# Gathering x in quarters of rows for three more slots of an attention and expert-layer kernel

## The chip, the core and the metric

The kernel runs on one core of one Trainium2 chip. The metric is the device time of one execution in microseconds (us), as a median over runs. Beside the timed runs there is one execution that the hardware profiler recorded, with the start and length of every instruction on each engine: PE (TensorE, matrix products), DVE (VectorE), ACT (ScalarE), POOL (GpSimd, which also issues the indirect DMAs) and SP (which issues the other DMAs). The program writes one list of instructions for each engine, in an order laid out by hand.

## The reference, cut to what matters

Attention over 8 batches of 576 tokens gives x, 4608 tokens of 512 numbers. Each token then goes to one of 8 experts, and its result is scaled by two gates:

```python
x = np.ascontiguousarray(attn_out.transpose(0, 2, 1, 3)).reshape(B * S, H * D)
...
logits = x @ w_gate
e_idx = np.argmax(logits, axis=1)
...
gate_w = probs[np.arange(N), e_idx]
eom = 1.0 / (1.0 + np.exp(-(x @ w_output_gate)))
...
for e in range(E):
    mask = e_idx == e
    ...
    h = np.maximum(x[mask] @ w1[e], 0.0)
    ye = h @ w2[e]
    out[mask] = gate_w[mask, None] * eom[mask, e, None] * ye
```

`probs` is the softmax of `logits`; w1 takes 512 numbers to 1024 and w2 takes them back.

## The kernel before, in words

**The attention** goes through four pairs of batches. Its x is stored to `xs` in device memory, 4608 rows of 576 numbers: four quarters of 144, each 128 numbers of x and 16 more of which one, written later, is the token's gate.

**The slots.** The expert layer is a list `order` of slots, counted here from 0 as in the code. Slots 0 to 9 take three blocks of 128 tokens each, slots 10 to 13 take two, and further ones, used only if the data needs them, take one. All blocks of a slot belong to one expert. Which tokens a slot takes is found on the chip while the attention still runs: list "a" (slots 0 and 1) after two pairs of batches, list "b" (slots 2 to 4) after three, list "l" (slots 5 and on) after the last. `table` (L213) makes a list: it ends with PE matmuls (L235), a copy `hl` of their result (L242), and the row numbers `idx_g` to gather x by (L249) and `idx_o` to store by (L252). For list "l" it goes on to `idx_q` (L259 to L274): four PE matmuls with the matrix `rep` (L262) spread the row numbers, and four DVE instructions (L267, L269, L272, L274) make from them the numbers of quarter rows. `rep` is made in `settle` (L1258, L1270), which runs once, when the slot with index `LAST` = 1 has been written out and the attention has been finished.

**The gather.** `gather` (L512) fetches a slot's x into a tile `xg`. A slot in `WHOLE` takes one indirect DMA for each block (L525), whole rows, one token on each partition. Any other slot has the flag `quart` and takes four for each block (L519), a quarter of a row each, laid out such that 32 by 32 transposes are enough. So three blocks take 3 issues in the first form and 12 in the second. Before the change `WHOLE` is slots 0 to 5. `gathers` (L587) issues gathers in order, up to two slots past the running one (three `xg` tiles), and only for slots whose flag `listed` is set; where a slot is needed at once (`must`) and is not listed, it calls `force` (L470), which writes out one more step of the list-making until it is.

**Turning x.** The matmuls need x with its columns on the partitions, split into a high and a low part. `turn_x(z, c)` (L1021) does one of four column chunks: for a whole-row slot three PE transposes into a PSUM bank (L1041), for a quarter slot one DVE transpose (L1035); then ACT makes the high part `xh` (L1043) and DVE the low part `xl` (L1044). At the first chunk of a quarter slot ACT also copies the gates out with four small copies (L1031). For slot i + 1 the four chunks are written in slot i, in the second half, after steps 1, 4, 6 and 9 of its 12 (`TURN`, `nxt` in `several`).

**One slot** (`several`, L1160): a first half of 8 matmul groups (L1176), each 12 matmuls into one bank, followed by ACT `hh` (L1181) and DVE `hl` (L1182); a second half of 12 steps of 6 matmuls (L1198) into three banks. As each of the three ends, `finish_y` (L1153) lets ACT scale it into a tile `y` (two buffers) and POOL store it with an indirect DMA (L1156). Weights come by DMA; `split` (L557) divides them into two parts with ACT (L564) and DVE (L565). From `settle` on, ten units of split weights can be held, and the slots' banks rotate through six.

**What else is written between them.** `hook` is called 8 times in the first half and once a step in the second, 20 times a slot. Each call first tries `gathers`, raises a clock by one once the attention is over, and writes two steps of the list-making (`late`): the ranking of the last tokens (`rank`, L875, with the masks `Aw` on POOL, L956), and `route_late` (L338) with list "l" behind it. `hold(n)` waits n ticks of that clock; `take_pr` waits for the one PSUM bank that all list-making shares, until its user clears `taken`.

Of the kernel before, what the change touches and what calls it, by code (L numbers as in the profile page):

```python
# [9 lines left out]
BF16 = mybir.dt.bfloat16  # L10
I32 = mybir.dt.int32
# [5 lines left out]
P = 128  # L17
# [12 lines left out]
NPE = sum(NPS)  # L30
NB3, NB2 = 3 * NPT, 2 * NPP
NBL = NB3 + NB2 + NSS
# [20 lines left out]
LATE = {"lg": 8, "w": 2, "pe": 3, "dve": 2}  # L53
# [1 line left out]
PUMP = (2, 1)  # L55
TURN = {3: (1, 4, 6, 9), 2: (1, 2, 4, 5)}
LAST = 1
WHOLE = tuple(range(NPE + 1))
XQ = 144
XROW = 4 * XQ  # L60

# [5 lines left out]
def attention_moe(tc, phiT, kv, qT, wgo, wall, out):  # L67
# [3 lines left out]
    with contextlib.ExitStack() as ctx:  # L71
        cp = ctx.enter_context(tc.tile_pool(name="cp", bufs=1))
# [20 lines left out]
        idx = {}  # L93
        for nm, n in (("a", 3 * NPS[0]), ("b", 3 * NPS[1]), ("l", NBL)):
            idx[nm] = (cp.tile([P, n], I32, name="idx_g" + nm), cp.tile([P, n], I32, name="idx_o" + nm),
                       cp.tile([P, 4, n], I32, name="idx_q" + nm) if nm == "l" else None)
        slot = cp.tile([P, NSLOT + 1], I32, name="slot")
        ctx.enter_context(tc.manual_schedule())
        ohcs = [cp.tile([P, E], BF16, name=f"ohc{i}") for i in range(NBP)]
# [4 lines left out]
        rt = ctx.enter_context(tc.tile_pool(name="rt", bufs=1))  # L104
# [108 lines left out]
        def table(nm, q, nch, nblk):  # L213

            while nm == "l" and "rl" not in env:
                yield
            bw = (env["rl"] if nm == "l" else rt).tile([P, nch, 2, nblk], BF16, name="bw" + nm)
            w = min(nch, 9 * NBL // nblk // 9 * 9)
            for c in range(0, nch, w):
                b3 = [P, w, nblk]  # L220
                eq = rt.tile([P, 9 * NBL], BF16, name="eq")
                eq = eq[:, 0:w * nblk].rearrange("p (c b) -> p c b", c=w)
                V.tensor_tensor(eq, iota_blk[:, 0:nblk].unsqueeze(1).to_broadcast(b3),
                                q[:, c:c + w].unsqueeze(2).to_broadcast(b3), ALU.is_equal)
                yield
                for i in range(2):
                    V.tensor_tensor(bw[:, c:c + w, i], eq,
                                    tok_hl[:, i, c:c + w].unsqueeze(2).to_broadcast(b3), ALU.mult)
                yield
            yield  # L230
            yield from take_pr()
            yield from hold(LATE["pe"])
            pi = ps_r.tile([P, 2, NBL], F32, name="pr")
            for c in range(nch):
                T.matmul(pi[:, :, 0:nblk], Aw[:, c], bw[:, c], start=(c == 0), stop=(c == nch - 1))  # L235
            yield
            yield from hold(LATE["dve"])
            hl = rt.tile([P, 2, NBL], BF16, name="hl_i")
            iv = rt.tile([P, NBL], F32, name="iv")
            i2 = rt.tile([P, NBL], F32, name="i2")  # L240
            ivv, i2v, hlv = iv[:, 0:nblk], i2[:, 0:nblk], hl[:, :, 0:nblk]
            V.tensor_copy(hlv, pi[:, :, 0:nblk])  # L242
            yield
            V.scalar_tensor_tensor(ivv, hlv[:, 0], 64.0, hlv[:, 1], ALU.mult, ALU.add)
            if nm != "l":
                taken.clear()
            yield
            ig, io, iq = idx[nm]
            V.tensor_scalar(ig[:], ivv, 1.0, 0.0, ALU.subtract, ALU.max)  # L249
            V.tensor_scalar(i2v, ivv, 0.0, 100000.0, ALU.is_equal, ALU.mult)  # L250
            yield
            V.scalar_tensor_tensor(io[:], ivv, -1.0, i2v, ALU.add, ALU.add)  # L252
            if nm != "l":
                return
            for z in order:
                if z["nm"] == nm and not z["quart"]:
                    z["listed"] = True

            rep = env["rep"]  # L259
            pq = ps_r.tile([P, 4, 2, NBL], F32, name="pr")  # L260
            for b in range(4):
                T.matmul(pq[:, b, :, 0:nblk], rep[:, b], hlv, start=True, stop=True)  # L262
            yield
            yield from hold(LATE["dve"])
            t4 = env["rl"].tile([P, 4, NBL], F32, name="iq")
            t4v = t4[:, :, 0:nblk]
            V.tensor_copy(t4v, pq[:, :, 1, 0:nblk])  # L267
            yield
            V.scalar_tensor_tensor(t4v, pq[:, :, 0, 0:nblk], 64.0, t4v, ALU.mult, ALU.add)  # L269
            taken.clear()  # L270
            yield
            V.tensor_scalar(t4v, t4v, 1.0, 0.0, ALU.subtract, ALU.max)  # L272
            yield
            V.tensor_scalar(iq[:], t4v, 4.0, quad[:, 0:1], ALU.mult, ALU.add)  # L274

        def counts(bp):
            pr = ps_r.tile([P, NCH, E], F32, name="pr")
# [3 lines left out]
        def route_early(k):  # L281

            nm, n, s0, nch = "ab"[k], NPS[k], sum(NPS[:k]), (k + 2) * NCH
# [46 lines left out]
            yield  # L330
            yield from table(nm, t1, nch, 3 * n)
            for z in order[s0:s0 + n]:
                z["listed"] = True
            if k == 0:
                gathers(0)
            yield
# [119 lines left out]
        def take_pr():  # L456

            while taken:
                yield
            taken.append(1)  # L460

        def hold(n):

            if "open" not in env:
                return
            end = clock[0] + n
            while clock[0] < end:
                yield
# [29 lines left out]
        for s in range(NSLOT):  # L498
            nb = 3 if s < NPE + NPT else 2 if s < NPE + NPT + NPP else 1
            if s < NPE:  # L500
                k = s >= NPS[0]
                nm, q0, rows = "ab"[k], 3 * (s - NPS[0] * k), (k + 2) * NCH * P
# [463 lines left out]
        def together(*gens):  # L966

            gens = [iter(g) for g in gens]
            while gens:
                for g in list(gens):  # L970
                    try:
                        next(g)
                    except StopIteration:
                        gens.remove(g)
                yield
# [159 lines left out]
        def grow(k):  # L1135
            for r, n in zip((ring, raw, xgs), GROW[k]):
                if n:
                    p = ctx.enter_context(tc.tile_pool(
                        name=f"{r.name}{k + 1}", bufs=n, reuse_waits="tile"))
                    r.add(p, n)  # L1140
# [117 lines left out]
        def settle():  # L1258

            att.finish()  # L1260
            pso.close()
            pa.close()
            env["hs"] = ctx.enter_context(tc.tile_pool(name="hs", bufs=1, side="right", reuse_waits="tile"))
            env["rl"] = ctx.enter_context(tc.tile_pool(name="rl", bufs=1, side="right", reuse_waits="tile"))
            env["xt"] = ctx.enter_context(tc.tile_pool(name="xt", bufs=2, side="right", reuse_waits="tile"))

            env["rep"] = env["rl"].tile([P, 4, P], BF16, name="rep")
            i4 = ident[:].rearrange("p (b i) -> p b i", b=4)
            for b in range(4):
                V.tensor_copy(env["rep"][:, b].rearrange("p (a i) -> p a i", a=4),  # L1270
                              i4[:, b:b + 1].to_broadcast([P, 4, 32]))
            grow(1)
            env["ps"] = ctx.enter_context(tc.tile_pool(name="p1", bufs=7 - NPK, space=PSUM, reuse_waits="tile"))

# [91 lines left out]
```

## Time and profile before

| | |
|---|---|
| Median of 3 timed runs | 578.89 us (578.73 to 579.51) |
| The profiled execution's own time | 577.36 us |
| Its span, first to last instruction | 575.6 us |
| Mean granted TensorE clock | 0.966 |
| Indirect gathers of whole rows | 18 issues |
| Indirect gathers of quarters | 80 issues |
| PE transposes of x (L1041) | 72 |

The profile's first part gives each engine's busy time. The timeline view lists instructions by start time, with their length, engine, line, operation and tiles, a count of merged instructions, and in brackets how long the engine had been idle and what ended that. The windows view gives busy time by stretch, with the granted PE clock. Views by line or by tile give counts, mean lengths, and for DMAs the time from issue to landing.

### The profile page before, as it was taken

Reading aid. Unit: us, or ns where it says so; the run is one execution under the profiler, and the core shown is the slowest. Engines: PE = TensorE matmul, PEld = TensorE weight load, DVE = VectorE, ACT = ScalarE, POOL = GpSimd, SP = SyncE. Lnnn points to the kernel's source line nnn. Section 1 sums busy time; section 2 is a strip of 40 time slices with the busy share of each in tenths; the row PEclk is TensorE's granted clock in tenths of the full one; section 3 lists DMA queues with packets and bytes.
Section 4 is the critical chain, followed back from the end, with each engine's and each line's share of the span. In section 5 each row is a group of like instructions: output and inputs, shape, how many; then the busy total and the mean of one; then the engine's idle time right before and its main releaser. Section 6 shows DMA issues by size and latency. Waiting matters only on the chain. (4 is left out here: it accounts for less than half of the span.)

```text
span 575.6 us, 10886 instructions
## 1 busy us (share of the span) xinstructions
PE 529.1 (92%) x4031; PEld 455.6 (79%) x4031; DVE 356.1 (62%) x736; ACT 280.4 (49%) x496; POOL 229.2 (40%) x253
## 2 busy tenths in 40 slices
PE   3688886789899999999999999999999999999993
PEld 2455554478689799898998989898998989899893
DVE  4485979767765659996443555646465555676610
ACT  3475655454254456453434545445454445656510
POOL 2242575831166034312471735547170604553011
PEclk9987879989899999999999999999999999999998
DMA  8999999975367659756564665656465655687000
GB/s 308 413 401 391 382 376 356 308 301 168 116 197 245 209 173 308 246 155 183 161 200 145 204 177 180 184 171 176 139 202 168 179 172 181 198 264 223 7 28 32
DMA packets 42238, 124.14 MB, mean 216 GB/s; under 512 B 10368, under 2 KB 10432, under 8 KB 41792
## 3 DMA queue, kind: packets, MB, share of 16 engines
q1 hardware_dynamic: 35136, 102.71, 54.7%
q0 software_dynamic: 7040, 20.65, 10.4%
q8 instruction: 33, 0.54, 0.4%
q14 instruction: 29, 0.24, 0.1%
HBM read 102.99 MB, written 20.87 MB: 215 GB/s over the span
## 5 line engine op out<-in xcount | busy, mean ns | idle before, releaser
L1176 PE MATMUL bps<-xh,whl 128*128 128x384 f32 (+1 forms) x896 | 213.6, 322 | 0.1
L1198 PE MATMUL bps<-whl,hh 128*128 128x512 f32 x608 | 197.7, 396 | 0.0
L565 DVE TENSOR_TENSOR whl<-w,whl 128x1024 fp32r<-128x1024 f32 x112 | 136.8, 1228 | 68.5 <-ACT whl L564 68.5
L1176 PEld LDWEIGHTS bps<-xh,whl 128*128 128x128 f32 x896 | 156.9, 190 | 1.9 <-issue 0.6
L1176 PE MATMUL bps<-xl,whl 128*128 128x384 f32 (+1 forms) x448 | 143.8, 321 | 0.0
L1198 PEld LDWEIGHTS bps<-whl,hh 128*128 128x128 f32 x608 | 114.7, 189 | 26.1 <-issue 2.5
L1198 PE MATMUL bps<-whl,hl 128*128 128x512 f32 x304 | 119.0, 391 | 0.0
L564 ACT CAST whl<-w 128x1024 fp32r<-128x1024 f32 x112 | 116.4, 1046 | 0.0
L519 POOL DMA_INDIRECT xg<-xs,idx_ql x80 | 90.2, 1127 | 25.2 <-issue 24.3
L1181 ACT ACTIVATE hh<-bps 128x384 fp32r<-128x384 f32 (+1 forms) x96 | 48.9, 510 | 96.9 <-PE bps L1176 96.7
L1182 DVE SCALAR_TENSOR_TENSOR hl<-bps,hh 128x384 fp32r<-128x384 f32 (+1 forms) x96 | 55.1, 577 | 52.1 <-ACT hh L1181 52.1
L1176 PEld LDWEIGHTS bps<-xl,whl 128*128 128x128 f32 x448 | 85.1, 190 | 0.5
L1156 POOL DMA_INDIRECT out<-y,idx_ol x23 | 24.9, 1081 | 127.1 <-ACT y L1155 101.4
L1198 PEld LDWEIGHTS bps<-whl,hl 128*128 128x128 f32 x304 | 57.5, 189 | 10.8
L838 POOL TENSOR_TENSOR ea<-ea,mx 128x512 f32<-128x512 f32 (+1 forms) x20 | 19.2, 961 | 49.8 <-DVE mx L836 45.4
L1043 ACT CAST xh<-xt 128x384 fp32r<-128x384 f32 (+1 forms) x32 | 14.7, 460 | 37.9 <-DVE xt L1035 37.9
L873 ACT COPY xo<-bpd 128x576 f32<-128x576 f32 x36 | 22.6, 640 | 21.3 <-PE bpd L871 12.7
L956 POOL TENSOR_SCALAR Aw<-iota_row,row 128x128 bf16<-128x128 bf16 x36 | 26.8, 759 | 12.4 <-DVE row L946 12.4
L871 PE MATMUL bpd<-ve_b,aT 64*128 64x144 f32 (+1 forms) x320 | 28.5, 327 | 2.4 <-DVE ea L833 2.4
L1044 DVE TENSOR_TENSOR xl<-xt,xh 128x384 fp32r<-128x384 f32 (+1 forms) x32 | 15.8, 492 | 24.1 <-ACT xh L1043 24.1
L1155 ACT ACTIVATE y<-bps,gx 128x512 f32<-128x512 f32 x20 | 13.4, 687 | 30.4 <-PE bps L1198 13.9
L871 PEld LDWEIGHTS bpd<-ve_b,aT 64*128 64x128 f32 (+1 forms) x320 | 21.7, 196 | 8.1 <-issue 3.5
(248 smaller groups left out, 471.6 us busy)
## 6 DMA issues: line engine op xcount, KB each, us to landing
w<-wall SPq DMA_DIRECT2D x112, 512.0 KB, 3.9
kvt<-kv SPq DMA_DIRECT2D x32, 512.0 KB, 7.5
xs<-xo SPq DMA_DIRECT2D x16, 576.0 KB, 5.8
qt<-qT SPq DMA_DIRECT2D x16, 512.0 KB, 9.1
ph<-phiT SPq DMA_DIRECT2D x3, 1152.0 KB, 12.1
kv<-kv SPq DMA_DIRECT2D x4, 512.0 KB, 9.0
xg<-xs,idx_ql POOLq DMA_INDIRECT x80, 4.2
ph<-phiT SPq DMA_DIRECT2D x4, 288.0 KB, 3.2
```

Source lines behind the costliest of these rows:

```text
L519: G.indirect_dma_start(out=z["xg"][:, k, XQ * b:XQ * b + XQ], out_offset=None, in_=xs[0:z["rows"]].rearrange("t (a q) -> (t a) q", a=4), i ...
L564: A.copy(hl[:, 0], w[:])
L565: V.tensor_tensor(hl[:, 1], w[:], hl[:, 0].bitcast(F32), ALU.subtract)
L838: G.tensor_tensor(eav, eav, mx[:, 0:n].unsqueeze(2).to_broadcast([P, n, M]), ALU.subtract)
L871: T.matmul(px[to:to + n, r, sl], z["aT"][h, o:o + n], ves[2 * bp + b][h, g], start=True, stop=True)
L873: A.copy(xo[:, c % 2], px[:, :, 0:2 * XQ])
L956: (G if AWP else V).tensor_scalar(Aw[:, bp * NCH + c], iota_row[:], row[:, c:c + 1], None, ALU.is_equal)
L1156: G.indirect_dma_start(out=out, out_offset=bass.IndirectOffsetOnAxis(ap=z["idx"][1][:, z["q0"] + k:z["q0"] + k + 1], axis=0), in_=y[:], in ...
L1176: T.matmul(pb[:, j % pb.shape[1], 0:n_], w[:, b, o:o + P], x[a][:, cc, 0:n_], start=(n == 0), stop=(n == 11))
L1181: A.activation(h_[:, js, 0:n_], pb[:, :, 0:n_], AF.Relu)
L1182: V.scalar_tensor_tensor(l_[:, js, 0:n_], pb[:, :, 0:n_], 0.0, h_[:, js, 0:n_].bitcast(F32), ALU.max, ALU.subtract)
L1198: T.matmul(py[k], h[u - 4][a][:, f, k * P:(k + 1) * P], w[:, b, DM * f:DM * f + DM], start=(u == 4 and f == 0 and n == 0), stop=(u == 7 an ...
```

## The change

Slots 3, 4 and 5 (the fourth to the sixth) become quarter slots too, so `WHOLE` is now 0, 1, 2. List "b" gets its own `idx_q`. The making of quarter numbers, until now the tail of `table`, becomes a generator `quarters(nm, hlv)` of its own. For list "l" it is still run at the end of `table`. For list "b" it needs `rep`, so `settle` puts it beside the ranking that is then under way (`together` lets each of the two go one step at a time), and the copy `hl` of list "b", in a tile of its own, is kept for it. A quarter slot is `listed` only when its quarter numbers have been written out.

```diff
-WHOLE = tuple(range(NPE + 1))
+WHOLE = (0, 1, 2)
...
-                       cp.tile([P, 4, n], I32, name="idx_q" + nm) if nm == "l" else None)
+                       cp.tile([P, 4, n], I32, name="idx_q" + nm) if nm != "a" else None)
...
-            hl = rt.tile([P, 2, NBL], BF16, name="hl_i")
+            hl = rt.tile([P, 2, nblk], BF16, name="hl_i" + nm)
...
             V.scalar_tensor_tensor(io[:], ivv, -1.0, i2v, ALU.add, ALU.add)
+            if nm == "b":
+                hls[nm] = hlv
             if nm != "l":
                 return
             for z in order:
                 if z["nm"] == nm and not z["quart"]:
                     z["listed"] = True
-
+            yield from quarters(nm, hlv)
+
+        hls = {}
+
+        def quarters(nm, hlv=None):
+
+            if hlv is None:
+                yield from take_pr()
+                yield from hold(LATE["pe"])
+                hlv = hls[nm]
+            iq, nblk = idx[nm][2], hlv.shape[2]
             rep = env["rep"]
             pq = ps_r.tile([P, 4, 2, NBL], F32, name="pr")
             for b in range(4):
...
             V.tensor_scalar(iq[:], t4v, 4.0, quad[:, 0:1], ALU.mult, ALU.add)
+            for z in order:
+                if z["nm"] == nm:
+                    z["listed"] = True
...
             for z in order[s0:s0 + n]:
-                z["listed"] = True
+                z["listed"] = z["listed"] or not z["quart"]
...
+            late.gens[0:1] = [together(quarters("b"), *late.gens[0:1])]
             grow(1)
```

## The prediction

> **What bounds the kernel now.** I read the engines' busy times first, then the windows view over the stretch that the change touches, then the timeline of each engine there.
>
> ```profile
> span 575.6 us, 10886 instructions
> PE 529.1 (92%) x4031; PEld 455.6 (79%) x4031; DVE 356.1 (62%) x736; ACT 280.4 (49%) x496; POOL 229.2 (40%) x253
> 212.00:248.50 36.50, 36.50 (x193) 33.30 (x192) 35.11 (x102) 21.48 (x32) 15.67 (x16) 1.00 0.82 268
> ```
>
> The last line is, roughly, slot 2: start and end, length, then busy time of PE, PEld, DVE, ACT and POOL, and the granted clock. PE has no gap, so a PE instruction less is time less. But DVE is busy for 35.11 of these 36.50 us as well (whole-kernel share: 62%), because `late` makes list "l" there.
>
> ```profile
> 241.22 0.33 PE L1176 MATMUL bps<-xh,whl 128*128 128x384 f32 x1
> 277.48 0.33 PE L1176 MATMUL bps<-xh,whl 128*128 128x384 f32 x1
> 308.90 0.49 PE L1041 MATMUL bps<-ident,xg 128*128 128x128 f32 x3
> 311.98 0.33 PE L1176 MATMUL bps<-xh,whl 128*128 128x384 f32 x1
> 345.01 0.33 PE L1176 MATMUL bps<-xh,whl 128*128 128x384 f32 x1
> ```
>
> The L1176 rows are the first matmuls of slots 3, 4, 5 and 6. Slot 5 already turns a quarter slot, slot 6: 345.01 - 311.98 = 33.03 us. Slot 4 turns a whole-row slot with four groups of PE transposes: 34.50. Slot 3 has those and list "l"'s matmuls: 36.26, so 1.76 for the list.
>
> **What it takes away.** The four groups for slots 3, 4 and 5, which stand in slots 2, 3 and 4: 34.50 - 33.03 = 1.47 us each, 4.4 in all. A group shows 0.49 us, but matmuls overlap, so I take the difference of slot times. In the Trainium skill, page "VectorE: DVE Perf Modes", section "The three transpose paths", a 128x128 transpose is put at 390 ns on TensorE, and the page's rules advise TensorE for it, which speaks against the change. By 390 ns the 24 transposes of slots 3 and 4 would free 9.4 us, not 2.9, and my sum would be 6.4 lower; the trace disagrees, with three of them in 0.49 us.
>
> **What it adds: when slot 3's x arrives.** The order of writing decides.
>
> ```profile
> 210.05 0.63 DVE L1270 CAST rep<-ident 128x128 bf16<-128x128 f32 x4
> 220.48 0.23 DVE L934 TENSOR_TENSOR w__2746<-ohg,pr 128x72 f32<-128x72 bf16 x1
> 229.19 0.24 DVE L186 TENSOR_SCALAR slot<-cs 128x4 int32<-128x4 f32 x1
> 229.27 0.55 DVE L1044 TENSOR_TENSOR xl<-bps,xh 128x384 fp32r<-128x384 f32 x1
> 241.95 0.55 DVE L1044 TENSOR_TENSOR xl<-bps,xh 128x384 fp32r<-128x384 f32 x1
> 271.46 0.33 DVE L267 COPY iq<-pr 128x180 f32<-128x180 f32 x1
> 272.50 0.32 DVE L274 TENSOR_SCALAR idx_ql<-iq,quad 128x180 int32<-128x180 f32 x1
> ```
>
> `settle` stands at 210.05 (the `rep` copies). `quarters("b")` starts there, but the shared bank is taken by `rank` until L934, written in slot 2's 5th hook. In that hook's second step `quarters` takes it; hold(3) puts its PE matmuls into hook 8 and hold(2) its first DVE instruction into hook 10, which is step 1 of the second half. Right behind that hook `nxt(0)` asks for slot 3's x, finds it not listed, and forces the last two steps. So the four DVE instructions come just ahead of where L1044 stood at 229.27. At most 0.33 us each and nearer 0.2 (36 elements a partition, not 180), and two of `late`'s steps forced along, 0.6: quarter numbers at about 230.8. Their four PE matmuls fall in slot 2, into idle time as will be seen: nothing. Then `gathers` writes out slot 3's 12 issues and, as slot 4 is listed too, its 12.
>
> ```profile
> 224.62 9.05 POOL L956 TENSOR_SCALAR Aw<-iota_row,row 128x128 bf16<-128x128 bf16 x9 [7.71 <-DVE row L946]
> 239.31 1.09 POOL L1156 DMA_INDIRECT out<-y,idx_ob  x1 [5.64 <-ACT y L1155]
> 285.70 1.04 POOL L519 DMA_INDIRECT xg<-xs,idx_ql  x1 [0.30 <-issue]
> ...
> 301.31 1.00 POOL L519 DMA_INDIRECT xg<-xs,idx_ql  x1 [0.30 <-issue]
> L519 POOL DMA_INDIRECT xg<-xs,idx_ql x80 | 90.2, 1127 | 25.2 <-issue 24.3
> L525 POOL DMA_INDIRECT xg<-xs,idx_gb x9 | 11.3, 1255 | 5.5 <-DVE idx_ob L252 3.1 <-issue 2.4
> DMA to landing us min/median/max: 2.5/4.2/8.1
> ```
>
> On POOL the gathers queue behind the nine masks, which end at 233.67. A quarter issue costs POOL 1127 ns against 1255 for a whole one: the price is by count. Twelve stand from 285.70 to 301.31, 1.42 us apart. So they run from 233.97, the last starts at 249.58, and with 4.2 us to landing x is there at 253.8 (252.1 to 257.7 by the ends). The page "DMA: Bandwidth & Descriptors" of the Trainium skill, section "Anatomy of one DMA", has a fixed 2.0 us plus the bytes at 436 GB/s, which for a quarter's 72 KB makes 2.2; that would bring everything 2.0 earlier, but the smallest landing in the trace is 2.5. PE wants this x at 241.22 - 1.47 = 239.75.
>
> **What stands behind that wait.** Slot 3's first DVE transpose is written at DVE's place of 229.27, and ACT's gate copies at ACT's matching place; both engines stop there until 253.8, with all that is written behind.
>
> ```profile
> 331.45 0.57 DVE L1035 STREAM_TRANSPOSE xt<-xg 128x384 f32<-128x384 f32 x1
> 332.66 0.56 DVE L1044 TENSOR_TENSOR xl<-xt,xh 128x384 fp32r<-128x384 f32 x1 [0.64 <-ACT xh L1043]
> 338.01 0.57 DVE L1035 STREAM_TRANSPOSE xt<-xg 128x384 f32<-128x384 f32 x1
> 229.83:241.95 12.12, 11.91 (x32) 1.00 0.79 262
> ```
>
> One chunk takes DVE 1.77 us from L1035 to the end of L1044 (331.45 to 333.22), 1.21 more than L1044 alone: chunk 0 is ready at 255.6. From the end of the first L1044 to the end of the fourth (229.83 to 242.51) DVE needed 12.68 us before, busy for 11.91 of the first 12.12: list steps and weight splits, with no slack. They must all still run, so chunk 3 is ready at 255.6 + 12.7 + 3 x 1.21 = 271.9, less 0.1 for list steps that changed places: 271.8. By then 10 of the 12 matmuls of slot 3's first group can be done (a group takes 2.09 us, as the next slots' halves of 8 groups show below); two, 0.35 us, are left. PE stands as if slot 3 had begun at 271.8 + 0.35 - 2.09 = 270.1, against 241.22: **+28.8 us**. The bounds: nothing if DVE weren't the last (a rival), and 3.9 more with the slowest landing. ACT has less than half of DVE's work in that stretch and isn't last. Weights don't lack: the program writes two splits a unit in slot 2's first half, which covers its second half and three units of slot 3 before DVE stops.
>
> **A second wait, in slot 4.** Slot 5's x now needs quarter numbers of list "l", 12 issues for 3. The two forced steps put all later list steps one hook earlier. L267 to L274 stood in hooks 16 and 17 of slot 3; now 15 and 16, so `gathers` writes the 12 in hook 17, step 8, ahead of slot 3's first store (step 9).
>
> ```profile
> 328.65 0.39 PE L1198 MATMUL bps<-whl,hh 128*128 128x512 f32 x1
> 343.51 1.02 POOL L1156 DMA_INDIRECT out<-y,idx_ol  x1 [7.79 <-ACT y L1155]
> 346.38 0.69 ACT L1155 ACTIVATE y<-bps,xg 128x512 f32<-128x512 f32 x1 [1.79 <-DMA out<-y,idx_ol]
> ```
>
> A first half takes 328.65 - 311.98 = 16.67 us, 2.09 a group. Slot 3 then starts at 270.1 and lasts 36.26 - 1.47 = 34.79, to 304.9. Its third chunk's transpose stands 26.0 into a quarter slot (338.01 - 311.98); with the chunk 1.77, two list instructions 0.57 and the 1.76 for the list, the numbers come at 270.1 + 30.1 = 300.2. POOL issues from 300.5 to 317.1, and the store of the first `y` starts at 317.4. The third `y` of a slot waits for that store (two buffers): it starts 2.87 us behind it (343.51 to 346.38), and ends 0.69 later, 321.0. Until then ACT makes no `hh`, and the third result's bank is not free. Of the six banks in rotation five are free by then, three that the first half used and two whose `y` is written: PE does five groups of slot 4, to 304.9 + 10.45 = 315.4, and stands still for **5.6 us**. This hangs on one hook: were the gathers written behind the first store, nothing. I take 5.6, with 0 and about 9 as ends. Slot 4's gathers, which delay slot 2's stores, cost nothing more: they end near 268, before DVE's 271.8.
>
> **The clock.**
>
> ```profile
> 25.00:30.00 5.00, 1.10 (x33) 0.52 (x33) 4.93 (x10) 2.78 (x8) 2.63 (x3) 0.77 1.03 416
> 30.00:35.00 5.00, 4.19 (x34) 2.43 (x36) 4.29 (x11) 3.35 (x8) 2.71 (x4) 0.55 1.02 406
> ```
>
> Where PE was nearly idle early on, the granted clock fell to 0.77 and 0.55; of the busy time there 1.10 x 0.23 + 4.19 x 0.45 = 2.1 us were lost. I add 2.1 behind the first wait and, between nothing and that, 1.0 behind the second: 3.1.
>
> **The sum**, against the profiled execution's 577.36: + 28.8 - 1.47 (slot 3) - 1.47 + 5.6 (slot 4) + 3.1 = 611.9. Slot 2's own 1.47 is lost in the wait. The median stands 1.5 above that execution, so I forecast **613 us**.
>
> **Rivals.** (1) *Faster: x comes in time.* Then 4.4 are saved and the four matmuls cost at most 0.3: 577.36 - 4.1 + 1.5 = 575. Chunk 3 would have to be ready by 241.5 (239.75 + 2.09 - 0.35): with DVE's queue as it is, the first gather would start by 204 (241.5 - 18.0 - 4.2 - 15.6), without that queue by 215. For it: POOL is 40% busy. Against: `rep` stands at 210.05, the bank is held until 220.48. 5%. (2) *Only the first wait*, since the stores get ahead of slot 5's gathers: 613 - 5.6 - 1.0 = 606. One hook decides. 14%. (3) *The landing alone decides*, DVE's queued work having no part: four chunks of 1.77 behind 253.8, 10.9 less, 602. The busy 11.91 of 12.12 speaks against it. 8%. (4) *The transposes also wait for slot 4's twelve issues*, on the same queue: 12 x 1.42 = 17 more, 630. 5%. (5) *The change does nothing that counts*, slot 3 being listed as before: 579, 2%; the flags speak against it.
>
> **How the numbers follow.** The forecast's own case keeps 66%. Landing at 2.5, no clock loss and no second wait would give 613 - 1.7 - 3.1 - 5.6 = 603; landing at 8.1, full clock loss (1.1 more) and a second wait of 9 give 621. From 602 to 621 the range holds cases one to three but for tails, about 8 in 10. Faster by over 0.2% (about what a measurement of this kernel can tell from no change) 5%, the same 2%, slower 93%.
>
> **What would show it.** Right: `idx_qb` on DVE near 230.8, 24 quarter issues on POOL from 234 to 268, L1035 on DVE near 254, PE idle from about 240 to 270 but for single matmuls, `y` of slot 4's predecessor waiting for a store near 320, and slots of 33.0 us from slot 5 on. Wrong: gathers starting before 215, or slot 3's first matmuls before 250.

## The result, and the profile after

| | before | after |
|---|---|---|
| Median of the timed runs | 578.93 us (578.73 to 579.51) | 613.55 us (612.69 to 614.52, 4 runs) |
| Ratio, with its 95% interval | | 1.0597 (1.0574 to 1.0620) |
| The profiled execution's own time | 577.36 us | 614.39 us |
| Its span | 575.6 us | 612.7 us |
| Mean granted TensorE clock | 0.966 | 0.932 |

The ratios, here and below, are taken over fast runs alone and are not simply the quotients of the medians beside them. The kernel became 6% slower, 34.6 us in the medians and 37.0 between the two profiled executions. The engines' busy times of the page after:

```profile
span 612.7 us, 10912 instructions
PE 533.8 (87%) x3999; PEld 458.8 (75%) x3999; DVE 362.5 (59%) x752; ACT 281.6 (46%) x508; POOL 259.7 (42%) x280
```

PE has 32 instructions less (4031 before): 36 transposes went and 4 small matmuls came. DVE and ACT have hardly more work, 6.4 and 1.2 us, POOL 30.5. PE, with fewer instructions, is busy only 4.7 us longer, so the rest of the 37 us is PE standing still. The view of waits between 225 and 325 us says which; its columns are the waiting engine, tile and line, what it waited for, then us in total, how often, and the longest.

```profile
DVE whl L580 <- ACT whl L579: 23.9, 3, 18.7
ACT gx L1046 <- DMA xg<-xs,idx_qb: 22.4, 4, 19.2
PE bps L1191 <- ACT xh L1058: 21.0, 4, 10.2
DVE xt L1050 <- DMA xg<-xs,idx_qb: 18.9, 1, 18.9
ACT y L1170 <- DMA out<-y,idx_ob: 17.0, 1, 17.0
```

There are two waits. In the first, ACT (19.2) and DVE (18.9) both stand at slot 3's quarter gather, and PE waits four times for a chunk of x. In the second, ACT stands at a `y` whose buffer a store has not left yet (17.0), and DVE stands behind ACT (18.7, in the first row). The timeline of POOL shows what came before each:

```profile
226.25 7.25 POOL L971 TENSOR_SCALAR Aw<-iota_row,row 128x128 bf16<-128x128 bf16 x9 [12.18 <-DVE row L961]
233.66 1.13 POOL L534 DMA_INDIRECT xg<-xs,idx_qb  x1 [0.16 <-PE bps L1213]
...
248.09 0.99 POOL L534 DMA_INDIRECT xg<-xs,idx_qb  x1 [0.30 <-issue]
...
267.03 1.00 POOL L534 DMA_INDIRECT xg<-xs,idx_qb  x1 [0.30 <-issue]
268.33 1.02 POOL L1171 DMA_INDIRECT out<-y,idx_ob  x1 [0.30 <-ACT y L1170]
301.41 1.27 POOL L534 DMA_INDIRECT xg<-xs,idx_ql  x1 [22.27 <-PE bps L1213]
...
316.28 1.00 POOL L534 DMA_INDIRECT xg<-xs,idx_ql  x1 [0.30 <-issue]
317.58 1.02 POOL L1171 DMA_INDIRECT out<-y,idx_ob  x1 [0.30 <-issue]
```

The 233.66, 248.09 and 267.03 rows are the first, the twelfth and the last of the 24 gathers for slots 3 and 4; 301.41 and 316.28 are the first and last for slot 5, and 317.58 is slot 3's first store, behind all of them. DVE's timeline, with the last of list "b"'s quarter numbers, the first chunk's transpose, the fourth chunk's low part, and list "l"'s numbers:

```profile
231.30 0.26 DVE L286 TENSOR_SCALAR idx_qb<-iq,quad 128x36 int32<-128x36 f32 x1
...
250.73 0.58 DVE L1050 STREAM_TRANSPOSE xt<-xg 128x384 f32<-128x384 f32 x1 [18.92 <-DMA xg<-xs,idx_qb]
...
267.47 0.56 DVE L1059 TENSOR_TENSOR xl<-xt,xh 128x384 fp32r<-128x384 f32 x1 [0.58 <-ACT xh L1058]
...
300.31 0.32 DVE L286 TENSOR_SCALAR idx_ql<-iq,quad 128x180 int32<-128x180 f32 x1
```

DVE starts the transpose 2.64 us behind the twelfth issue, not behind the 24th. On PE's timeline slot 2 ends at 241.72, slot 3's first matmuls come in drips as chunks arrive, and a second gap of 6.69 us lies in slot 4:

```profile
241.33 0.39 PE L1213 MATMUL bps<-whl,hh 128*128 128x512 f32 x1
251.90 0.69 PE L1191 MATMUL bps<-xh,whl 128*128 128x384 f32 x1 [10.19 <-ACT xh L1058]
...
257.49 0.69 PE L1191 MATMUL bps<-xh,whl 128*128 128x384 f32 x1 [3.98 <-ACT xh L1058]
...
262.25 0.69 PE L1191 MATMUL bps<-xh,whl 128*128 128x384 f32 x1 [3.17 <-ACT xh L1058]
...
267.49 0.69 PE L1191 MATMUL bps<-xh,whl 128*128 128x384 f32 x1 [3.64 <-ACT xh L1058]
...
303.92 0.33 PE L1191 MATMUL bps<-xh,whl 128*128 128x384 f32 x1
...
321.20 0.69 PE L1191 MATMUL bps<-xh,whl 128*128 128x384 f32 x1 [6.69 <-ACT y L1170]
...
345.50 0.33 PE L1191 MATMUL bps<-xh,whl 128*128 128x384 f32 x1
```

The bracket at 321.20 names the `y` that the wait was for; ACT's timeline has it, 2.88 us behind the store at 317.58:

```profile
320.46 0.69 ACT L1170 ACTIVATE y<-bps,gx 128x512 f32<-128x512 f32 x1 [16.96 <-DMA out<-y,idx_ob]
```

Last the windows, with busy PE, PEld, DVE, ACT and POOL and then the granted clock. After:

```profile
253.00:262.00 9.00, 2.11 (x5) 0.79 (x3) 7.97 (x18) 3.47 (x5) 7.30 (x6) 0.50 0.61 189
262.00:272.00 10.00, 6.11 (x16) 4.99 (x17) 7.00 (x22) 2.84 (x5) 6.01 (x5) 0.50 0.60 193
272.00:277.00 5.00, 5.00 (x26) 5.00 (x26) 2.32 (x5) 3.72 (x6) 1.00 (x1) 0.86 0.22 65
311.00:325.00 14.00, 7.31 (x34) 6.99 (x33) 2.88 (x4) 4.54 (x8) 7.31 (x8) 0.76 0.27 76
207.94:303.92 95.98, 75.01 (x391) 65.48 (x390) 62.86 (x161) 37.60 (x61) 42.67 (x40) 0.86 0.52 158
```

The last line is slots 2 and 3 whole, 95.98 us. Before, they took 71.19 (from 206.29 to 277.48), so 24.79 went there. In PE's starts the whole of the loss can be booked: slot 2 starts 1.65 later than before (207.94 against 206.29), slots 2 and 3 take 24.79 more, slot 4 takes 41.58 against 34.50 (7.08 more), slots 5 and on take the same (slot 5 33.02, before 33.03; the last slot starts at 577.89 against 544.38, which is the 33.5 of these three), and the end of the program, from the start of the last slot, takes 3.5 more. Together 37.0, the difference of the spans.

### The profile page after: what moved, and what is told of

Read it like the earlier page. It is cut to its first block, busy times and chain, and to the rows that moved or that the text cites. A ratio compares the mean times of both kernels' runs of the same rounds, so it can differ in the third digit from the quotient of the medians.

```text
span 612.7 us, 10912 instructions
## 1 busy us (share of the span) xinstructions
PE 533.8 (87%) x3999; PEld 458.8 (75%) x3999; DVE 362.5 (59%) x752; ACT 281.6 (46%) x508; POOL 259.7 (42%) x280
## 5 line engine op out<-in xcount | busy, mean ns | idle before, releaser
L1191 PE MATMUL bps<-xh,whl 128*128 128x384 f32 (+1 forms) x896 | 219.6, 328 | 27.7 <-ACT xh L1058 21.0
L1213 PE MATMUL bps<-whl,hh 128*128 128x512 f32 x608 | 194.2, 393 | 0.0
L1191 PEld LDWEIGHTS bps<-xh,whl 128*128 128x128 f32 x896 | 160.6, 194 | 31.3 <-ACT xh L1058 22.9
L1191 PE MATMUL bps<-xl,whl 128*128 128x384 f32 (+1 forms) x448 | 146.7, 328 | 0.0
L534 POOL DMA_INDIRECT xg<-xs,idx_ql x92 | 105.0, 1141 | 50.0 <-issue 27.1
L1191 PEld LDWEIGHTS bps<-xl,whl 128*128 128x128 f32 x448 | 86.9, 194 | 1.7 <-DVE xl L1059 1.2
L1058 ACT CAST xh<-xt 128x384 fp32r<-128x384 f32 (+1 forms) x44 | 20.8, 473 | 60.0 <-DVE xt L1050 59.8
L1170 ACT ACTIVATE y<-bps,gx 128x512 f32<-128x512 f32 x29 | 19.6, 687 | 58.3 <-PE bps L1213 26.9
L1059 DVE TENSOR_TENSOR xl<-xt,xh 128x384 fp32r<-128x384 f32 (+1 forms) x44 | 22.4, 510 | 32.3 <-ACT xh L1058 32.3
L853 POOL TENSOR_TENSOR ea<-ea,mx 128x512 f32<-128x512 f32 (+1 forms) x20 | 19.2, 961 | 46.8 <-DVE mx L851 42.5
L1050 DVE STREAM_TRANSPOSE xt<-xg 128x384 f32<-128x384 f32 (+1 forms) x44 | 23.0, 523 | 18.9 <-DMA xg<-xs,idx_qb 18.9
```

The source lines that it names most:

```text
L534: G.indirect_dma_start(out=z["xg"][:, k, XQ * b:XQ * b + XQ], out_offset=None, in_=xs[0:z["rows"]].rearrange("t (a q) -> (t a) q", a=4), i ...
L1050: V.transpose(xt[:, 0:n].rearrange("p (k i) -> p k i", i=32), xg[:, 0:nb].rearrange("p k (b q) -> p (k b) q", b=4)[:, :, 32 * c:32 * c + 32])
L1191: T.matmul(pb[:, j % pb.shape[1], 0:n_], w[:, b, o:o + P], x[a][:, cc, 0:n_], start=(n == 0), stop=(n == 11))
L1213: T.matmul(py[k], h[u - 4][a][:, f, k * P:(k + 1) * P], w[:, b, DM * f:DM * f + DM], start=(u == 4 and f == 0 and n == 0), stop=(u == 7 an ...
```

## The experiments

The theory behind the forecast: (a) slot 3's x comes late, DVE and ACT stop in front of it, and the work queued on DVE behind that point sets when slot 3 can run; (b) slot 5's twelve issues get ahead of slot 3's first store; (c) a PE transpose group less is worth 1.47 us where nothing waits. Rivals: the landing alone decides; slot 4's issues matter; the clock is most of it. Each kernel was timed beside the kernel before on the same chip; the four chips differ (578.52 to 580.98 for the kernel before), so rows of different chips are best compared by their ratios. Slot lengths are those of one profiled execution of each kernel. Slots are numbered from 0, and a slot's time runs from PE's first matmul in it to the next slot's.

| Run | time, us | before there | ratio (95%) |
|---|---|---|---|
| slots 3 and 4 alone | 605.42 | 579.42 | 1.0455 (1.0421 to 1.0488) |
| slot 5 alone | 578.74 | 579.42 | 0.9999 (0.9975 to 1.0023) |
| slot 5 alone, numbers two steps earlier | 583.57 | 579.42 | 1.0084 (1.0057 to 1.0111) |
| the change, slot 3's chunks together | 611.40 | 579.42 | 1.0555 (1.0524 to 1.0587) |
| the change, slot 4's gathers held back | 617.82 | 578.52 | 1.0673 (1.0632 to 1.0714) |
| the change, PE kept busy in the wait | 613.31 | 578.52 | 1.0603 (1.0563 to 1.0642) |
| list "b"'s quarter numbers made early | 599.01 | 578.52 | 1.0350 (1.0304 to 1.0397) |
| early numbers, chunks together | 598.67 | 578.52 | 1.0332 (1.0279 to 1.0384) |
| the change, chunks late | 608.55 | 580.98 | 1.0442 (1.0392 to 1.0491) |
| early numbers, a step taken off POOL | 598.70 | 580.98 | 1.0259 (1.0203 to 1.0315) |
| slot 4 alone, early numbers | 583.34 | 580.98 | 1.0053 (1.0015 to 1.0092) |
| the same, PE matmuls held back | 582.73 | 580.29 | 1.0042 (1.0017 to 1.0068) |

### One part of the change at a time

**Slots 3 and 4 alone.** The lines taken out and put in are against the change, here and below:

```diff
-WHOLE = (0, 1, 2)
+WHOLE = (0, 1, 2, 5)
```

> Only slots 3 and 4 gather quarters; slot 5 keeps whole rows. My theory: the changed kernel has two separate waits, a first one for slot 3's x and a second one in slot 4 that slot 5's twelve gathers cause, since they stand on POOL ahead of slot 3's stores. Without them the second wait goes: in the changed kernel slot 4 lasts 41.58 us against 33.03, so 8.6 go, and 1.5 come back for slot 5's PE transposes. 613.5 - 8.6 + 1.5 = 606.4. Rival: the second wait is an after-effect of the first (engines that run late); then it stays, and the time is 615.

It took 605.42. Slots 2 and 3 still take 95.82 us (206.38 to 302.20), slot 4 takes 34.50 as before the change. So the first wait is whole without the second, and the second hangs on slot 5 being a quarter slot: both as forecast.

**Slot 5 alone.**

```diff
-WHOLE = (0, 1, 2)
+WHOLE = (0, 1, 2, 3, 4)
...
-            late.gens[0:1] = [together(quarters("b"), *late.gens[0:1])]
```

> Only slot 5 gathers quarters, and list b gets no quarter numbers, so no step of the list-making is forced. My theory: the numbers for slot 5 come in hook 17 of slot 3, its gathers are written in hook 18, behind the first store, and nothing waits: 578.9 - 1.5 (one slot's PE transposes) = 577.4. Rival: twelve gathers near the stores hold them up in any case; then 577.4 + 8.6 = 586.

578.74: no difference. Slot 4 does take 33.03 instead of 34.50, so the group of transposes is worth 1.47. It is given back: slot 5 takes 34.15 (1.12 more), slot 8 33.78 (0.75 more), and 0.8 comes behind the last store (the last section). Of slot 5's 1.12 the profile puts 0.5 down to waits for an `hl` and a `y`; where the rest and slot 8's 0.75 come from is not shown. POOL's timeline here has the first store ahead of the gathers:

```profile
275.32 0.97 POOL L1171 DMA_INDIRECT out<-y,idx_ob  x1 [26.34 <-ACT y L1170]
276.60 1.06 POOL L534 DMA_INDIRECT xg<-xs,idx_ql  x1 [0.30 <-issue]
...
317.44 1.02 POOL L1171 DMA_INDIRECT out<-y,idx_ob  x1 [0.30 <-issue]
```

There is no second wait in slot 4. The row at 317.44 is slot 4's own store, delayed by slot 6's gathers.

**Slot 5 alone, two list steps earlier.** The same kernel, with the two steps forced that the change forces:

```diff
+                        if i == 2 and c == 0:
+                            force()
+                            force()
                         gathers(i, i + 2)
```

> As the run with slot 5 alone, but two steps of the list-making are forced in slot 2, where the changed kernel forces two. My theory: that puts slot 5's gathers one hook earlier, ahead of slot 3's first store, and brings the second wait without the first: 577.4 + 8.6 = 586, with a gap on PE of 6 to 7 us in slot 4. Rival (the wait comes from lateness left over from the first wait): no gap, 577.4.

583.57, with a PE gap of 4.28 us in slot 4, which takes 39.13. POOL's timeline has the order turned round:

```profile
273.35 1.28 POOL L534 DMA_INDIRECT xg<-xs,idx_ql  x1 [23.82 <-DVE idx_ql L286]
...
289.26 1.02 POOL L1171 DMA_INDIRECT out<-y,idx_ob  x1 [0.30 <-issue]
```

So two list steps, written one hook earlier, make the second wait by themselves: the mechanism is shown without slot 3 having any part. Its price here, 4.8 us in the medians of the two runs, is below the expected 8.6, and below the change's.

### What sets the first wait

**Chunks together.** If the list steps and splits between the chunks hold them up, four chunks in a row should be ready 11 us earlier:

```diff
-                if step in TURN[nb]:
+                if i == 2 and step == 1:
+                    for c in range(4):
+                        nxt(c)
+                elif i != 2 and step in TURN[nb]:
```

> The changed kernel, with the four chunks of slot 3's x written one behind the other after step 1 of slot 2, ahead of DVE's queued list steps and weight splits. My theory: of the first wait only the arrival of x at about 250.6 counts then, plus four chunks of 1.73, 257.5 instead of 268.0 for the last; 10.5 less, 603. Rival: DVE's queued work has no part (arrival and a cold PE alone): 613 as before. Another: the splits, now behind, hold PE up in slot 3 and give half of it back: 608.

A miss: 611.40. DVE's timeline has the first transpose where it was, and the fourth low part at 256.94 instead of 267.47, as expected:

```profile
250.89 0.58 DVE L1050 STREAM_TRANSPOSE xt<-xg 128x384 f32<-128x384 f32 x1 [19.06 <-DMA xg<-xs,idx_qb]
...
256.94 0.56 DVE L1059 TENSOR_TENSOR xl<-xt,xh 128x384 fp32r<-128x384 f32 x1 [0.58 <-ACT xh L1058]
```

Yet slots 2 and 3 take 95.55, against 95.98 in the change. The windows from 257 to 287, first of the change and then of this run:

```profile
257.00:287.00 30.00, 22.71 (x101) 20.34 (x101) 23.34 (x54) 14.29 (x22) 13.10 (x10) 0.73 0.56 174
```

```profile
257.00:287.00 30.00, 22.35 (x132) 20.41 (x133) 27.61 (x63) 15.13 (x25) 10.03 (x9) 0.90 0.61 184
```

DVE (the third busy time) is at 27.61 of 30 in this run. The work that had stood between the chunks now stands behind them, and PE waits for it there, in several gaps between 1 and 2.2 us: for the list's tables (3.8 us at L235), for an `hl` (1.0), and 2.8 for nothing that the profile names. The 2 us by which this run is faster lie in slot 4 (39.23 against 41.58). So what costs in slots 2 and 3 is that DVE stood still for 19 us with work for all of them; in which order it catches up matters little here.

**Slot 4's gathers held back** until slot 3, so that slot 2's stores stand ahead of them on POOL:

```diff
                 z = order[gat[0]]
+                if gat[0] == 4 and i < 3:
+                    break
```

> The changed kernel, but slot 4's twelve gathers are not written before slot 3's first hook, so that slot 2's stores stand ahead of them on POOL. My theory: they cost nothing in the changed kernel, since slot 2's stores are late for another reason (ACT waits for slot 3's x): 613.5, within 1. Rival: the late stores of slot 2 hold ACT and so PE at the start of slot 3, or the transposes wait for all 24 gathers: 3 to 17 less.

A miss: 617.82. Now slot 4's x comes late too. DVE's timeline:

```profile
250.10 0.58 DVE L1052 STREAM_TRANSPOSE xt<-xg 128x384 f32<-128x384 f32 x1 [19.21 <-DMA xg<-xs,idx_qb]
...
295.34 0.58 DVE L1052 STREAM_TRANSPOSE xt<-xg 128x384 f32<-128x384 f32 x1 [7.78 <-DMA xg<-xs,idx_qb]
```

DVE stands 7.78 us more, and slots 2 and 3 take 104.07, 8.1 more than in the change. That slot 4's issues delay the stores of slot 2 was not a cost; having them early was needed.

**Chunks late.** The chunks of slots 3 and 4 are written together after step 8, so that DVE works off its list steps and splits first; slot 4's gathers are held back as above.

```diff
-                if step in TURN[nb]:
+                if i in (2, 3):
+                    if step == 1:
+                        gathers(i, i + 2)
+                    if step == 8:
+                        for c in range(4):
+                            nxt(c)
+                elif step in TURN[nb]:
```

> The changed kernel with its gathers at their places, but in slots 2 and 3 the four chunks for the next slot are written after step 8 of the second half, behind most of DVE's list steps and splits, and slot 4's gathers stand behind slot 2's stores. My theory as the runs so far have left it: what the first wait costs is DVE's dead time (18.9 us in the changed kernel) in a stretch in which DVE has no room, so the order behind the wait changes nothing, but work put ahead of it does. DVE then works on until about 243, x comes at 250.7, the last chunk is ready at 257.5: about 11 less, 602, with slot 4's own lateness as the doubt (up to 4). Rival: the wait itself, not DVE's idle time, sets the loss: 611 as with the chunks written together.

608.55, a gain, but about half of what was expected in slots 2 and 3. DVE's timeline there:

```profile
254.15 0.58 DVE L1052 STREAM_TRANSPOSE xt<-xg 128x384 f32<-128x384 f32 x1 [13.41 <-DMA xg<-xs,idx_qb]
```

DVE had work until 240.74, not 243, and x came at 254.15, not 250.7: it stood still for 13.41 us where the expectation comes to 7.7. That is 5.5 us less than in the change, and slots 2 and 3 take 90.83, 5.15 less. Slot 4 takes 39.12, and in this one profile slots 6, 7, 11 and 12 take 3.4 more together, for which no cause is shown. Over these runs the length of slots 2 and 3 follows DVE's idle time at the gather: 13.4 goes with 90.8, 18.9 with 96.0, 19.1 (chunks together) with 95.6, 27.0 (19.2 and 7.8) with 104.1. It does not follow the arrival of x: here x came 3.4 later than in the change, and the two slots were shorter.

**PE kept busy.** In slot 3's first group PE gets 40 dummy matmuls before the first chunk and 11 before each of the others, into a bank nobody reads:

```diff
                         for cc in range(4):
+                            if i == 3 and u == 0 and j == 0:
+                                if cc == 0:
+                                    pf = bank([512], "ps")
+                                for _ in range(11 if cc else 40):
+                                    T.matmul(pf, w[:, 0, 0:P], w[:, 0, 0:512], start=True, stop=True)
```

> The changed kernel with 40 + 3 x 11 extra matmuls into an unused bank, placed in PE's four gaps of the first wait (their result is not used). They are to keep the granted clock up, and by the durations seen they are shorter than the gaps. My theory: about 6 us of full work behind the wait run at half clock in the changed kernel (to 273.4), so 3 us go: 610.5. Rival: the low clock costs nothing there, since PE waits for DVE and ACT anyway: 613.5.

613.31, no gain that can be told. The granted clock is now 1.00 where it was 0.50, and slots 2 and 3 take 94.51, 1.47 less. But slot 4 takes 42.28, 0.70 more. The window, and the row on PE that ends the second wait:

```profile
253.00:272.00 19.00, 14.02 (x64) 11.01 (x63) 14.11 (x40) 7.28 (x11) 13.68 (x11) 1.00 0.58 187
318.48 0.69 PE L1196 MATMUL bps<-xh,whl 128*128 128x384 f32 x1 [6.69 <-ACT y L1170]
```

The second wait is as long as in the change, 6.69, and counted from the start of slot 2 it ends 1.46 earlier. What is lost again lies behind it: the granted clock is 0.50 in the 4.5 us after that row (318.48 to 323.00), where the change had 0.62 (321.20 to 325.70). At the start of slot 5 this run is 0.8 ahead, counted the same way.

### Can the saving be kept?

**Early numbers.** List "b"'s quarter numbers are made with the list itself, in slot 1, with a copy of `rep` in a spare part of the masks' tile, instead of in `settle`:

```diff
-            if nm != "l":
+            if nm == "a":
                 return
...
+            if nm == "l":
+                rep = env["rep"]
+            else:
+                rep = Aw[:, 27:31]
...
-            late.gens[0:1] = [together(quarters("b"), *late.gens[0:1])]
```

> Slots 3, 4 and 5 gather quarters, but list b's quarter numbers are made together with list b, while the attention runs, so that x is there in time. My theory: then DVE is what binds in slot 2: it was busy for 35.11 of 36.50 us, and four chunks by DVE transposes take 4.8 more, so the last chunk is ready near 247.3 where PE wants it at 241.5. PE loses 5.8 in slot 2 of the 4.4 that the three slots save: 580, at most 1.5 above before. Rival (DVE has room): 574.5.

A miss: 599.01. The wait in front of slot 3 is gone, but slot 1 takes 52.42 us (before 38.12). POOL's timeline there:

```profile
193.66 0.99 POOL L539 DMA_INDIRECT xg<-xs,idx_qb  x1 [11.52 <-issue]
...
208.56 1.00 POOL L539 DMA_INDIRECT xg<-xs,idx_qb  x1 [0.30 <-issue]
209.58 0.32 POOL L920 TENSOR_TENSOR w__2789<-lg,lm 128x72 f32<-128x72 f32 x1
```

and ACT's:

```profile
209.94 0.26 ACT L930 ACTIVATE w__2789<-w__2789 128x72 f32<-128x72 f32 x1 [10.53 <-POOL w__2789 L920]
```

The ranking of the last tokens has one subtraction on POOL (L920). It now stands behind slot 3's twelve issues, and ACT stands behind it for 10.53 us. PE's waits in slot 1 are two lines, the second of them for the copies of `rep`:

```profile
PE bps L1061 <- DVE xl L1064: 6.1, 1, 6.1
PE pr L279 <- DVE Aw L275: 3.1, 1, 3.1
```

The other 5.1 of the 14.3 us that slot 1 lost are PE being busy longer, 43.28 us against 38.12, at a granted clock of 0.87 against 1.00. Behind it, slots 2 to 4 take 109.67, 4.0 more than before, where the expectation was 1.4: PE waits 4.9 there for parts `xh` of slot 3's x.

**Early numbers, chunks together.** The edits of the last kernel and of the one with the chunks together.

> As the run with early numbers, and slot 3's four chunks written together after step 1 of slot 2, ahead of DVE's list steps. My theory: the chunks are ready near 236, in time, and the list steps have room behind: the full 4.4 are saved, 574.5. Rival (DVE's total work in slots 2 and 3 binds, wherever the chunks stand): 578 to 580.

A miss for the same reason, 598.67, with slot 1 at 52.37. Behind it slot 2 takes 33.42 (34.93 before: the saving is there), slot 3 41.28 (36.26 before), where PE waits 3.8 for DVE's list tables.

**Early numbers, a step taken off POOL.** As the last, with the subtraction on DVE, and the copies for `rep` made at the start of the table:

```diff
-            G.tensor_tensor(w2_[:], lt, lmb, ALU.subtract)
+            (V if bp == NBP - 1 else G).tensor_tensor(w2_[:], lt, lmb, ALU.subtract)
```

> As the run with early numbers and chunks together; the matrix for the numbers is made some steps earlier, and the last ranking's subtraction, which stood behind the twelve gathers on POOL, is done on DVE. My theory: the 14.4 us lost in slot 1 go, and DVE's extra work shows as a wait of PE for list l's table in slot 3 (3.8 us before, with the clock about 6): 580. Rival: slot 1's loss has another cause than POOL's queue: 594 or more. Another: everything fits: 574.5.

A miss: 598.70, on a chip where the kernel before took 580.98. Slot 1 takes 44.74, so 7.6 of the 14.3 us that it had lost went with these two edits, and ACT no longer waits for the subtraction. PE's waits there name 1.9 us for `hl_ib` and 2.7 for an `xl`; the other 2 of the 6.6 that stayed are PE being busy longer, 40.19 us against 38.12, at a granted clock of 0.96. So POOL's queue and the late copies were a part of slot 1's loss, and not all of it. Slots 2 and 3 take 80.90, 6.2 more than in the run before this one, with PE waiting for DVE's tables again (4.2): most of what slot 1 won is lost there.

**Slot 4 alone, early numbers.** Slots 3 and 5 go back to whole rows:

```diff
-WHOLE = (0, 1, 2)
+WHOLE = (0, 1, 2, 3, 5)
```

> Only slot 4 gathers quarters, with its numbers made early; its gathers are written in slot 2's first hook, and its DVE transposes fall in slot 3, where DVE was busy for 23.45 of 35.50 us. My theory: one slot's PE transposes are saved and nothing waits: 1.5 less than before, 577.5 against 579. Rival (the masks of the last ranking, now behind twelve gathers on POOL, come too late for list l's table): slower by some us.

583.34, and so 0.5% slower than before (0.15 to 0.92%). Slot 3 takes 34.95 instead of 36.26, a saving of 1.31. Slot 1 takes 40.34, 2.2 more, and the waits of PE in it are one line:

```profile
PE pr L277 <- DVE hl_ib L247: 1.8, 1, 1.8
```

Slot 8 takes 35.46 instead of 33.03, where PE waits 1.7 for an `xh`. The code there is as before.

**The same, PE's matmuls held back**, so that other attention work comes between `hl` and them:

```diff
+            if nm == "b":
+                yield from hold(LATE["pe"])
```

> As the run in which slot 4 alone has quarter gathers and the second list's quarter numbers are made with the first list's, but PE's matmuls for those numbers stand behind a hold, so that other attention work goes to PE while VectorE makes the copies they read. Theory: that run lost 2.2 us in slot 1 because PE waited there for VectorE's copy, and saved 1.3 us in slot 3; with the wait filled the saving of 1.3 to 1.5 us is left, about 1.5 us below the kernel before (ratio near 0.9975). Rival: the added work costs the attention its time on VectorE, GpSimd or PE whatever its order, or the quarter gathers delay slot 8 again: the same as before or up to 2.5 us above it.

582.73, ratio 1.0042. The hold does what it was meant to: PE has no wait in slot 1 any more, which takes 38.23, and slot 3 takes 34.95. The gain is still not there. Slot 1 starts 1.27 later than in the profile of before, slot 7 takes 1.09 and slot 11 2.45 more, and the end of the program 0.8 more. Ahead of slot 11, slot 10's last `hh` starts 2.9 us late on ACT, by the spacing of those before it (484.18, 487.06, then 492.84), and slot 11's x stands behind it; PE had begun slot 10's second half at 489.74, and what held the `hh` is not settled. The rival stands as far as the time goes. Why slots 7, 8 and 11 are longer in these two runs stays open, and since the record does not say on which chip the one profile of the kernel before was taken, the chip may have a part in it.

No kernel that was run beats the kernel before.

## Why the prediction was right, step by step

The forecast was 613 us, and 613.55 was measured. The direction held, and so did the second wait's mechanism. Of the first wait it held that slot 3's x comes late and that DVE, stopped in front of it, is what PE then lacks; that the order of DVE's backlog matters did not hold. That the sum came out within 1 us is luck: what was missing or too small in it comes to 7.1 us, and what was too large to 7.0.

**The saving of 1.47 a slot**: right. 1.47 in slot 4 with slot 5 alone, 1.31 in slot 3 with slot 4 alone. The transposes' price in the Trainium skill, page "VectorE: DVE Perf Modes", section "The three transpose paths", gives an estimate of 390 ns x 12 = 4.7 for one slot. Its figure is for bf16, and x is f32 here; these two runs speak for the row, not the page.

**The place of the quarter numbers**: right. They were forecast at about 230.8 and are there at 231.56; the stretch before slot 2 was 1.65 later in this execution, which the forecast did not have.

**The gathers**: 24 issues from 234 to 268 forecast, 233.66 to 268.03 measured. Spacing 1.42 forecast, (248.09 - 233.66) / 11 = 1.31 measured.

**The landing**: mis-sized. I took 4.2, the median of all gathers; DVE starts 2.64 behind the twelfth issue, near the lower end of 2.5. The row I had read, the twelve gathers from 285.70 on, ran with the DMA engines busy for 0.66 of the time. These twelve ran at 0.20 to 0.23 (233.66 to 250.73), while DVE and ACT stood still. The Trainium skill, page "DMA: Bandwidth & Descriptors", section "Anatomy of one DMA — SWDGE (gpsimd) path", has 2.0 fixed plus the bytes, an estimate of 2.2 for a quarter; here it was nearer than the row I took.

**The first wait, +28.8**: too large. By the forecast's own rule, chunk 3 ready at 268.03 makes slot 3 start as if at 268.03 + 0.35 - 2.09 = 266.3, which is 23.4 behind 241.22 + 1.65. Of the 5.4 that are missing, 1.6 is the landing, 1.2 the spacing, 0.7 the queue on DVE (17.3 from first transpose to fourth low part, not 18.0), and 1.96 that the masks were over at 233.50, in spite of the later start (233.66 against 233.97 + 1.65). The forecast's reading, that the queue between the chunks is what slot 3 waits for, was too narrow: with the chunks together that queue was gone from in front of slot 3, and the time stayed. As far as these runs show, it is DVE's total that counts from 231 on. The window that the forecast calls roughly slot 2 (212.00 to 248.50, DVE 35.11 of 36.50) reaches 7.3 us into slot 3; over slot 2 itself, 206.29 to 241.22, DVE is busy for 31.32 of 34.93. The sum does not use that row, but the expectation of the run with early numbers does.

**Slot 4's gathers cost nothing**: right, and more than that. Held back, they cost some 4 us.

**The second wait, 5.6**: right in kind, 6.69 measured. Its lower end, nothing, is the case of slot 5 alone, where the first store gets ahead. Five groups of slot 4 were forecast before the stop, and PE stops 10.6 us into it, which is five groups; the first row behind the stop is at 321.20, where 321.0 was forecast for the `y` that frees it.

**The clock, 3.1**: too small. Slots 2 and 3 are 303.92 - (266.3 + 34.79) = 2.8 longer than the first wait explains, and slot 4 is 7.08 + 1.47 - 6.69 = 1.9: 4.7, if all of it is the clock. The granted clock was 0.50 from 253 to 272 and 0.86 up to 277; in slot 4 it was 0.62 from 321.20 to 325.70, which is 1.7 us of the 1.9. The 2.1 behind the first wait had been carried over from another stretch, where PE's idle time looked otherwise, so its size was a guess. The Trainium skill, page "TensorE: Matmul & The Clock Gate", section "What's actually happening", has half clock after an idle window of about 3.4 us. The rows agree so far that idle stretches of 10.19, 3.98, 3.17 and 3.64 us go with a clock of 0.50; as one of them is shorter than that window, they do not test its length. The run with PE kept busy bounds it: with a clock of 1.00 in that stretch, slots 2 and 3 got 1.47 shorter, not 2.8. The other 1.3 has no cause that was shown.

**Slots of 33.0 from slot 5 on**: right, 33.02.

**Not forecast**: 1.65 before slot 2, and 3.5 from the last slot on. The first varies from run to run (slot 2 starts between 206.38 and 207.96 in five other kernels with the same program ahead of it), so it is not the change's as far as the runs show. The second is shown in the last section.

So the terms stand: first wait and its clock, less slot 3's saving, 29.4 forecast (28.8 - 1.47 + 2.1) and 24.79 measured; slot 4 5.1 (5.6 - 1.47 + 1.0) and 7.08; the two unforeseen terms 5.2. Against the profiled execution the forecast was 611.9 and 614.39 came out; the median, which I put 1.5 above that, lies 0.8 below it, and so the last digits agree by chance. Of the rivals, "only the first wait" at 606 is what slots 3 and 4 alone give, 605.42: its price was right, its condition did not hold here. That the transposes also wait for slot 4's issues is ruled out by the start 2.64 behind the twelfth, and that the landing alone decides by the run with the chunks together, which gave 611.40 and not 602.

## What to carry to other kernels

When an instruction is written ahead of its data, count not only its own lateness but all that is queued behind it on its in-order engine: here 19 us of standing still on DVE, at an engine that the whole-kernel share shows 62% busy, came back nearly one for one as time (5.5 us less of it were worth 5.15), and reordering the backlog behind the wait did not recover it; putting work ahead of the wait did, in part. An indirect DMA is priced by the issue: twelve held POOL for 16 us (301.41 to 317.28), and what stands behind them on that queue, a store or a small subtraction, is where the next wait comes from. A saving of 1.5 us that a trace shows in its own slot is a gain only if the next waits have slack for what moved.

## What the runs showed that I had not expected

**The end of the program grows with the number of indirect DMAs.** These are the last stores on POOL's timeline, before and after:

```profile
568.01 0.97 POOL L1156 DMA_INDIRECT out<-y,idx_ol  x1 [4.47 <-ACT y L1155]
```

```profile
601.66 0.98 POOL L1171 DMA_INDIRECT out<-y,idx_ol  x1 [4.60 <-ACT y L1170]
```

From the end of that row to the end of the span it is 6.7 us before (575.65 - 568.98) and 10.0 after (612.68 - 602.64), with only the landing of that store left to come, 3.0 and 3.2 us behind its start. Over all profiles it goes with the count of gathers: 98 issues 6.7; 107 issues 7.5 to 7.6 (four kernels); 116 issues 8.5; 125 issues 9.7 to 10.0 (eight kernels). So 27 issues more cost 3.0 to 3.4, some 0.12 us each, whichever slots they belong to and however long the kernel runs. That goes off every slot's saving of 1.47: nine issues more take about 1 us of it. Most of the growth lies in two instructions that POOL runs behind the last store; the traces hold them, but the views leave them out, as they are not counted as busy. `INC_SWDGE_SEM` lasts 0.80, 0.97, 1.16 and 1.33 us at 98, 107, 116 and 125 issues, and the `DRAIN` behind it 2.53, 3.27, 4.00 and 4.74, the same to 0.01 in every kernel of one count. Together that is 2.74 us more for the 27 issues, and the other engines' closing instructions come only behind this `DRAIN` (before, it ends at 574.80, and they go on at 574.98). Why it grows with the count the traces don't show.

**Idle DVE time against PE clock.** Filling PE's wait with dummy matmuls brought the granted clock from 0.50 to 1.00 and gave 1.47 us in its stretch. Of this 0.7 went again behind the second wait, where the clock came back later, and the 0.8 that were left cannot be told in the whole, 613.31 against 613.55.
